# Threshold attention and a bilinear feed-forward layer on one core: two small VectorE instructions take a second tensor operand

## The chip, the cores and the metric

The kernel runs on one core of a Trainium2 chip. The metric is the device time of one execution in microseconds (us). A core has a matrix engine (TensorE, PE in the profile, with its weight loads listed as PEld), a vector engine (VectorE, DVE), a scalar engine (ScalarE, ACT), a general engine (GpSimd, POOL) and a queue engine that starts transfers (SyncE, SP). They run side by side and wait for each other through semaphores. Data lie in SBUF, an on-chip memory of 128 partitions, and matrix products arrive in PSUM. [...]

## The reference

The attention has 8 batches, 8 heads, 576 positions and a head width of 64. Scores that lie more than `tau` below the greatest of their row are dropped, and the rest go through a softmax. The heads of a position, side by side, are a row `x` of 512 numbers for the feed-forward layer.

```python
scores = scale * np.matmul(q, k.transpose(0, 1, 3, 2))
thresh = np.max(scores, axis=-1, keepdims=True) - tau
scores = np.where(scores >= thresh, scores, -1000000000.0)
scores = scores - np.max(scores, axis=-1, keepdims=True)
attn = np.exp(scores)
attn = attn / (np.sum(attn, axis=-1, keepdims=True) + 1e-09)
attn_out = np.matmul(attn, v)
x = attn_out.transpose(0, 2, 1, 3).reshape(B * S, H * D)
out = (x @ w_a) * (x @ w_b) @ w_out
```

Here x has 4608 rows, and the hidden width of the layer is 1536. All of it is float32.

## The kernel before

**Units of attention.** Heads are taken in 32 pairs. For each pair the 576 rows of queries are cut into units: four of 128 rows for each of the two heads, and a tail (u = 4) in which the last 64 rows of both heads share one tile of 128 partitions. So a unit u < 4 has two tiles of scores, a tail unit has one. There are 160 units, 128 with two tiles and 32 with one.

**What a unit does.** `scores` has TensorE compute q times k into PSUM (L352), VectorE take the maximum of each row (L359, one instruction for each tile, one number per partition) and then, once for the unit, the threshold `thr` (L360) from the one or two maxima and the constant `cut`. `cut` is a column of `scalars`: tau in the units of the raw product, or a huge number if tau is negative. `weigh` has ScalarE make a bias from the maximum (L379) and the exponential (L380), and VectorE keep those whose score reaches the threshold and add up the row (L383), which leaves the row sums in `sums`. `reciprocal` adds 1e-9 to the one or two sums, on ScalarE (L392) in the eight units beside which weights are being converted and on VectorE (L394) in the others, and takes the reciprocal (L396). For the first eight units the reciprocals become diagonal matrices for TensorE (`diagonals`, `turn_pe`). For the others ScalarE multiplies the weights by them (`normalise`, L402), VectorE transposes blocks of 32 by 32 (L446), SP writes them to a scratch tensor in HBM (`swap`, L457) and reads them back as `wT` (L466, L469), and TensorE multiplies by v (`product`, L483).

**The feed-forward layer.** Its matrix products (L633, L706, L763, L809) are cut into small steps by a generator, and `advance` puts as many of them between the parts of each unit as a pace allows. Some products are replaced by fewer ones over sums of blocks. GpSimd computes these sums from tiles in SBUF: L513 of x, L582 and L594 of the weights, L732 of the hidden values and of results. It also copies halves of x across partitions (L506) and multiplies hidden values (L599). In the first 150 us GpSimd and VectorE convert the weights as well (L254, L260, L268, L273).

**What sets the order.** The main loop over units writes the instructions in the order in which each engine is to run them, and `keep_order` ties every instruction to the one before it on its engine. Nothing is reordered by a scheduler. Every engine and the SP queue run strictly in that order. On VectorE the threshold stands behind the two maxima of its unit; behind it come transposes of the unit before and the masking. The sums stand in front of the reciprocal on which L402 waits.

**What touches the lines of the change.** `mx`, `thr`, `sums` and `rcp` are small tiles in SBUF of two float32 numbers per partition, each with two buffers. L360 reads `mx` and the scalar `cut`; L394 reads and writes `sums`. In a tail unit only the first column is used.

Of the kernel before, what the change touches and what calls it, by code (L numbers as in the profile page):

```python
# [14 lines left out]
ALU = mybir.AluOpType  # L15
# [37 lines left out]
def kernel(  # L53
# [38 lines left out]
    nc = tc.nc  # L92
# [33 lines left out]
    def banks(n, name):  # L126

        return psum.tile([P, 2, 512], FP32, tag="banks", name=name)[:, :, 0:n]
# [175 lines left out]
    ok, e_scale, e_nscale, cut, big = (scalars[:, c:c + 1] for c in range(5))  # L304
# [35 lines left out]
    def scores(i, u):  # L340
        qT, kT = prepared[i]["q" if i < HP else "q1" if u > 1 else "q0"], prepared[i]["k"]
        base = HALF if i >= HP and u > 1 else 0
        n = 2 if u < NT else 1
        sc = [banks(SH, "sc") for _ in range(n)]
        each = [(c, t, j) for c in range(2) for t in range(n) for j in range(2)]
        if units.index((i, u)) < BY_HEAD:
            each.sort(key=lambda x: x[2])
        for c, t, j in each:
            r = slice(j * D, (j + 1) * D)
            o = t if u < NT else 1 - j  # L350
            q0, to = (u * P + t * D if u < NT else MAIN) - base, slice(o * D, (o + 1) * D)
            nc.tensor.matmul(sc[j if u < NT else 0][to, c], qT[r, q0:q0 + D],  # L352
                             kT[r, c * SH:(c + 1) * SH], start=True, stop=True)
        mx = small.tile([P, 2], FP32, tag="mx", name="mx")
        thr = small.tile([P, 2], FP32, tag="thr", name="thr")
        bias = small.tile([P, 2], FP32, tag="bias", name="bias")
        for j in range(n):
            c = slice(j, j + 1)
            nc.vector.tensor_reduce(mx[:, c], sc[j], axis=AX.XY, op=ALU.max)  # L359
        nc.vector.tensor_scalar(thr[:, 0:n], mx[:, 0:n], cut, None, op0=ALU.subtract)  # L360
        scored[i, u] = (sc, thr, bias, mx)

    def rooms_of(i, u):
# [24 lines left out]
    def reciprocal(i, u, engine):  # L388
        ws, sums = weights[i, u]
        n = len(ws)  # L390
        if engine is nc.scalar:
            nc.scalar.activation(sums[:, 0:n], sums[:, 0:n], AF.Copy, bias=1e-9)  # L392
        else:
            nc.vector.tensor_scalar_add(sums[:, 0:n], sums[:, 0:n], 1e-9)  # L394
        rcp = small.tile([P, 2], FP32, tag="rcp", name="rcp")
        nc.vector.reciprocal(rcp[:, 0:n], sums[:, 0:n])  # L396
        weights[i, u] = (ws, rcp)
# [522 lines left out]
    n = 0  # L920
# [4 lines left out]
    for g in range(len(units) + PV_LAG):  # L925
# [4 lines left out]
        if here:  # L930
            i, u = units[g]
            scores(i, u)
# [24 lines left out]
        if here and g < BY_PE:  # L957
            reciprocal(i, u, nc.vector)
# [8 lines left out]
        if g > BY_PE:  # L967
            advance(PORTIONS[1] * pace)
            n = g - PV_LAG
# [12 lines left out]
        if here and g < BY_PE:  # L982
            diagonals(i, u)
        elif here:
            reciprocal(i, u, nc.scalar if converting else nc.vector)
            normalise(i, u)
# [71 lines left out]
```

## Time and profile before

| | before |
|---|---|
| median of 3 runs | 1462.98 us (1459.54 to 1463.87) |
| profiled execution, its own time | 1467.37 us |
| its span, first to last instruction | 1465.6 us |
| TensorE busy | 1387.9 us (95%) |
| VectorE busy | 1014.9 us (69%) |
| ScalarE busy | 682.9 us (47%) |
| GpSimd busy | 479.5 us (33%) |
| L360 on VectorE | 160 instructions, 44.4 + 6.9 us |
| L394 on VectorE | 152 instructions, 30.0 + 4.9 us |
| mean granted TensorE clock | 0.994 |

The profile is of one execution. Busy time is the time in which an engine ran an instruction, whatever the instruction waited for inside itself: a wait for a semaphore counts as idle, [...]. The two parts of L360 and L394 are those of two numbers per partition and of one. In a line of a group, `out<-in` names the tiles, and after the count come the busy time, the mean of one instruction in nanoseconds, and the idle time just before.

### The profile page before, as it was taken

How to read it: one execution, taken by the hardware profiler on the slowest of the kernel's cores; microseconds unless marked ns; L12 is line 12 of the kernel's file. 1: busy time of each engine (PE TensorE's matmuls, PEld its weight loads, DVE VectorE, ACT ScalarE, POOL GpSimd, SP SyncE). 2: the span in 40 equal slices, each digit the busy share in tenths (PEclk: the TensorE clock that was granted, in tenths of full speed). 3: DMA queues.
4: the chain of work that ended last, by engine and by line, in shares of the span. 5: the costliest groups of instructions: out<-in, count | busy, mean ns of one | idle time of the engine just before them, and what ended most of it. 6: DMA issues, size and time to landing. Idle time of an engine off the chain costs nothing.

```text
span 1465.6 us, 76332 instructions
## 1 busy us (share of the span) xinstructions
PE 1387.9 (95%) x34208; PEld 1248.2 (85%) x34208; DVE 1014.9 (69%) x2245; ACT 682.9 (47%) x1243; POOL 479.5 (33%) x668
## 2 busy tenths in 40 slices
PE   5788999999999999999999899999999999999998
PEld 4677687987989889899998788998898979989997
DVE  6898688787767787586757677767767776755223
ACT  5787455545545554454444445444545455431110
POOL 2774713423060606033334224150606060605000
PEclk9999999999999999999999999999999999999999
DMA  9976677668756775577555766477656776450000
GB/s 217 227 207 181 155 183 190 167 169 189 195 135 160 165 203 145 137 174 180 142 135 138 163 165 169 121 177 167 173 147 144 179 188 165 122 148 30 4 17 17
DMA packets 325080, 223.21 MB, mean 152 GB/s; under 512 B 169616, under 2 KB 308880, under 8 KB 324752
## 3 DMA queue, kind: packets, MB, share of 16 engines
q1 hardware_dynamic: 322384, 217.73, 60.7%
q8 instruction: 269, 4.41, 1.3%
q10 hardware_dynamic: 2368, 0.59, 0.2%
q14 instruction: 59, 0.48, 0.1%
HBM read 128.58 MB, written 89.65 MB: 149 GB/s over the span
## 4 chain that ended last, share of the span: by engine, by line
PE 78%; DVE 7%; DMA 5%; SPq 5%; issue 3%; ACT 1%; POOL 1%; ACTq 0%; DVEq 0%; POOLq 0%
PE pab L633 24%; PE pab L706 18%; PE po L763 17%; PE pv L483 9%; PE sc L352 9%; DMA wT<-swap 2%; SPq L457 2%; DVE mx L359 2%; SPq L147 1%; DMA qT<-in_q_dram 1%; DVE tw L446 1%; DVE tw L383 1%; PE po L809 1%; SPq L225 1%; POOL kept L732 0%
## 5 line engine op out<-in xcount | busy, mean ns | idle before, releaser
L402 ACT ACTIVATE tw<-tw,rcp 128x576 f32<-128x576 f32 x272 | 197.8, 769 | 216.9 <-DVE rcp L396 216.8
L359 DVE TENSOR_REDUCE mx<-sc 128x1 f32<-128x576 f32 x288 | 205.6, 751 | 134.6 <-PE sc L352 131.3
L380 ACT ACTIVATE tw<-sc,bias,scalars 128x576 f32<-128x576 f32 x288 | 239.3, 831 | 9.8 <-DMA vm<-in_v_dram 0.2
L599 POOL TENSOR_TENSOR h<-h,u 128x512 f32<-128x512 f32 x28 | 35.1, 1272 | 621.8 <-DVE h L676 485.8
L383 DVE SCALAR_TENSOR_TENSOR tw<-sc,thr,tw 128x576 f32<-128x576 f32 x288 | 223.0, 798 | 14.0 <-ACT tw L380 13.8
L763 PE MATMUL po<-wo_sb,h 64*64 64x256 f32 x3264 | 222.9, 377 | 0.0
L352 PE MATMUL sc<-kT,qT 64*64 64x288 f32 x2016 | 192.0, 405 | 10.5 <-ACT xt L490 4.7
L446 DVE STREAM_TRANSPOSE tw<-tw 128x576 f32<-128x576 f32 x272 | 196.0, 754 | 0.8 <-ACT tw L402 0.8
L483 PE MATMUL pv<-wT,vm 64*64 64x160 f32 (+3 forms) x5184 | 182.4, 275 | 14.3 <-DMA wT<-swap 8.0
L763 PEld LDWEIGHTS po<-wo_sb,h 64*64 64x64 f32 x3264 | 167.4, 133 | 24.9
L483 PEld LDWEIGHTS pv<-wT,vm 64*64 64x64 f32 x5184 | 166.2, 135 | 25.3 <-issue 10.4
L763 PE MATMUL po<-sums_u,h 64*64 64x256 f32 x2448 | 163.9, 376 | 1.6 <-DVE h L714 1.6
L732 POOL TENSOR_TENSOR h<-h 128x256 f32<-128x256 f32 x168 | 117.4, 728 | 114.6 <-PE po L763 100.5
L352 PEld LDWEIGHTS sc<-kT,qT 64*64 64x64 f32 x2016 | 115.1, 133 | 32.5 <-ACT xt L490 12.3
L763 PEld LDWEIGHTS po<-sums_u,h 64*64 64x64 f32 x2448 | 123.4, 133 | 20.7 <-DVE h L714 2.3
L633 PE MATMUL pab<-xU,wb_sb 64*64 64x128 f32 x4096 | 133.5, 270 | 0.2 <-issue 0.2
L379 ACT ACTIVATE bias<-mx,scalars 128x1 f32<-128x1 f32 x288 | 83.0, 288 | 100.6 <-DVE mx L359 100.5
L633 PEld LDWEIGHTS pab<-xU,wb_sb 64*64 64x64 f32 x4096 | 127.6, 133 | 2.6 <-issue 0.5
L491 DVE COPY xT<-pv 64x128 f32<-64x128 f32 (+1 forms) x136 | 38.1, 280 | 120.3 <-PE pv L483 119.1
L633 PE MATMUL pab<-xS,wa_sb 64*64 64x128 f32 x2048 | 110.8, 270 | 3.2 <-POOL xS L506 2.0
L490 ACT COPY xT<-pv 128x128 f32<-128x128 f32 (+1 forms) x68 | 17.6, 258 | 206.0 <-PE pv L483 205.9
L706 PE MATMUL pab<-xS,wb_sb 64*64 64x256 f32 (+1 forms) x1536 | 99.9, 359 | 2.9 <-issue 2.9
(137 smaller groups left out, 2429.0 us busy)
## 6 DMA issues: line engine op xcount, KB each, us to landing
swap<-tw SPq DMA_DIRECT2D x480, 144.0 KB, 2.6
wT<-swap SPq DMA_DIRECT2D x120, 576.0 KB, 4.7
vm<-in_v_dram SPq DMA_DIRECT2D x128, 72.0 KB, 3.3
swap<-tw SPq DMA_DIRECT2D x128, 72.0 KB, 2.0
kT<-in_k_dram SPq DMA_DIRECT2D x112, 72.0 KB, 4.3
wT<-swap SPq DMA_DIRECT2D x56, 144.0 KB, 2.9
out_dram<-kept SPq DMA_DIRECT2D x30, 256.0 KB, 4.0
qT<-in_q_dram SPq DMA_DIRECT2D x112, 40.0 KB, 4.5
```

The lines of the kernel that those rows point to most:

```text
L352: nc.tensor.matmul(sc[j if u < NT else 0][to, c], qT[r, q0:q0 + D], kT[r, c * SH:(c + 1) * SH], start=True, stop=True)
L359: nc.vector.tensor_reduce(mx[:, c], sc[j], axis=AX.XY, op=ALU.max)
L379: nc.scalar.activation(bias[:, j:j + 1], mx[:, j:j + 1], AF.Copy, scale=e_nscale)
L380: nc.scalar.activation(wb[j], sb[j], AF.Exp, bias=bias[:, j:j + 1], scale=e_scale)
L383: nc.vector.scalar_tensor_tensor(out=wv, in0=sb[j], scalar=thr[:, j:j + 1], in1=wv, op0=ALU.is_ge, op1=ALU.mult, accum_out=sums[:, j:j + 1])
L402: nc.scalar.activation(w, w, AF.Copy, scale=rcp[:, j:j + 1])
L446: nc.vector.transpose(w, w)
L483: nc.tensor.matmul(pv[c * D:(c + 1) * D, y], vm[rows, s], wT[y](rows, s), start=(s == 0), stop=(s == NSLOT - 1))
L633: nc.tensor.matmul(out[c * D:(c + 1) * D, r, f * P:(f + 1) * P], w[g][k][rows, w0:w0 + D], moving[k][rows], start=(fresh and k == 0 and f ...
L706: nc.tensor.matmul(pab[c * D:(c + 1) * D, r], w[rows, f // n, k, fs + c * D:fs + (c + 1) * D], moving, start=(k == 0), stop=(k == H - 1))
L732: (nc.vector if state["over"] else nc.gpsimd).tensor_tensor(*a, **kw)
L763: nc.tensor.matmul(po[c * D:(c + 1) * D, r, y], ht[rows, t0:t0 + D], other[rows, f], start=(f == 0), stop=(f == NF // 2 - 1))
```

## The change

The threshold and the sum plus 1e-9 are computed by `scalar_tensor_tensor` in place of `tensor_scalar`. That instruction computes (in0 op0 scalar) op1 in1. The second tensor operand is the same tile as the first. The threshold is min(mx − cut, mx), which is mx − cut because `cut` is not negative. The sum is max(sums + 1e-9, sums), which is sums + 1e-9. Both second operands lie in SBUF.

```diff
-        nc.vector.tensor_scalar(thr[:, 0:n], mx[:, 0:n], cut, None, op0=ALU.subtract)
+        nc.vector.scalar_tensor_tensor(out=thr[:, 0:n], in0=mx[:, 0:n], scalar=cut, in1=mx[:, 0:n],
+                                       op0=ALU.subtract, op1=ALU.min)
...
         if engine is nc.scalar:
             nc.scalar.activation(sums[:, 0:n], sums[:, 0:n], AF.Copy, bias=1e-9)
         else:
-            nc.vector.tensor_scalar_add(sums[:, 0:n], sums[:, 0:n], 1e-9)
+            nc.vector.scalar_tensor_tensor(out=sums[:, 0:n], in0=sums[:, 0:n], scalar=1e-9, in1=sums[:, 0:n],
+                                           op0=ALU.add, op1=ALU.max)
```

The lines that follow move down, L383 to L384, L396 to L398 and so on; the threshold stays at L360, and the sum becomes L395. Each engine has the same instructions in the same order as before, with the same semaphores.

## The prediction

> **What bounds the kernel now.** I read the page from the top: busy time by engine, then the chain of work that ended last. From it, these lines are the ones that matter here (microseconds busy, share of the span, instructions; then shares of the chain):
>
> ```profile
> span 1465.6 us, 76332 instructions
> PE 1387.9 (95%) x34208; PEld 1248.2 (85%) x34208; DVE 1014.9 (69%) x2245; ACT 682.9 (47%) x1243; POOL 479.5 (33%) x668
> ...
> PE 78%; DVE 7%; DMA 5%; SPq 5%; issue 3%; ACT 1%; POOL 1%; ACTq 0%; DVEq 0%; POOLq 0%
> ```
>
> TensorE sets the time: it is busy 95% of the span and is 78% of the chain. VectorE (DVE) has 31% of its span free and carries only 7% of the chain, some 100 us. A microsecond saved or added on DVE is therefore worth much less than a microsecond, except where the chain runs through it.
>
> The second view is DVE's groups with each shape apart (count, busy us, mean ns). The change rewrites the L360 and L394 groups; L396, L260 and L268 are there for comparison:
>
> ```profile
> L360 DVE TENSOR_SCALAR thr<-mx,scalars 128x2 f32<-128x2 f32 x128 | 44.4, 347 | 4.5
> L394 DVE TENSOR_SCALAR sums<-sums 128x2 f32<-128x2 f32 x120 | 30.0, 250 | 2.0
> L396 DVE RECIPROCAL rcp<-sums 128x2 f32<-128x2 f32 x128 | 21.2, 166 | 6.6 <-ACT sums L392 2.4
> L260 DVE SCALAR_TENSOR_TENSOR low<-raw,low 128x512 uint32<-128x512 uint32 x13 | 9.2, 709 | 0.1
> L268 DVE TENSOR_SCALAR wa_sb<-wa_sb 128x512 uint32<-128x512 uint32 x12 | 7.7, 639 | 0.0
> L360 DVE TENSOR_SCALAR thr<-mx,scalars 128x1 f32<-128x1 f32 x32 | 6.9, 214 | 1.1
> L394 DVE TENSOR_SCALAR sums<-sums 128x1 f32<-128x1 f32 x32 | 4.9, 154 | 1.0
> ```
>
> Two elements per partition cost 347 ns where one costs 214, and 250 where one costs 154. Width cannot explain that: the reciprocal costs 166 and 164 ns. The answer for L360's own instances gives 212/228/1849 ns as least, median and greatest, so most are short and some are very long.
>
> The third view is the order of time, DVE and GpSimd (POOL) side by side (start us, us). A long two-wide threshold, and a one-wide one in the same position:
>
> ```profile
> 268.90 1.85 DVE L360 TENSOR_SCALAR thr<-mx,scalars 128x2 f32<-128x2 f32 x1
> 268.36 4.69 POOL L594 TENSOR_TENSOR wb_sb<-wa_sb,wb_sb 128x1024 f32<-128x1024 f32 x2
> 784.14 0.21 DVE L360 TENSOR_SCALAR thr<-mx,scalars 128x1 f32<-128x1 f32 x1
> 782.40 2.49 POOL L599 TENSOR_TENSOR h<-h,u 128x512 f32<-128x512 f32 x2 [38.04 <-DVE h L676]
> ```
>
> The two-wide one starts in the first of two POOL instructions and ends at 270.75, just after that one ends (half of 4.69 us from 268.36 is 270.7). The one-wide one runs inside a POOL instruction and takes its plain 0.21 us. Going through all instances this way, 38 of the 128 two-wide thresholds and 35 of the 120 two-wide sums meet a running POOL instruction long enough to hold them. Together they last 15.2 and 10.8 us longer than their medians (228 and 168 ns): 26 us of DVE time. No one-wide instance is lengthened.
>
> [...] only the two-wide form waits. [...] the new form has two SBUF inputs. The trace has such instructions on DVE already:
>
> ```profile
> 100.74 1.12 DVE L260 SCALAR_TENSOR_TENSOR low<-sums_u,low 128x512 uint32<-128x512 uint32 x1
> 100.13 1.19 POOL L254 TENSOR_SCALAR wo_sb<-wo_sb 128x512 f32<-128x512 f32 x2
> 1332.11 7.56 DVE L732 TENSOR_TENSOR h<-h 128x256 f32<-128x256 f32 x9 [0.72 <-PE po L763]
> 1335.33 0.91 POOL L513 TENSOR_TENSOR xU<-xS 128x256 f32<-128x256 f32 x1
> ```
>
> L260 is the very instruction kind that the change uses. Undisturbed it takes 683 ns (its median); here it takes 1.12 us, and POOL's pair of instructions ends at 101.32. It waited 0.44 us, which is POOL's end (0.58 us after its start) less 0.14 us. Three other cases of L260 and twelve of L732 fit the same rule to within about 10 ns (L732: up to 950 ns for a plain 417). The present sums follow it too (1099 ns with POOL's end 1074 ns after the start: 931 waited, 143 less); the thresholds wait POOL's end less 0.20 us. [...] the waits of old and new form are alike.
>
> **The change part by part.** Counts: 160 thresholds (128 two-wide, 32 one-wide) and 152 sums (120 and 32). No instruction, wait or transfer is added or moved, and the order on every engine stays; the eight sums done on ScalarE (L392) are untouched.
>
> 1. *Plain cost.* [...] I take the new forms at these one-wide figures: 228 to 214 and 168 to 154, one-wide ones unchanged. That is 248 × 14 ns = 3.5 us less on DVE. Bounds: no gain below that is in sight; [...] If the second operand cost another 60 ns each, 312 × 60 = 19 us would be added to DVE.
> 2. *Waits of the two-wide forms.* They stay: 26 us before, 26 us after. Lower end: all 26 us go, if a two-element read slips past. I take the upper one, on L260 and L732.
> 3. *Waits of the one-wide forms.* New. Laying the rule (POOL's end less 0.20 us, less 0.14 us) on the one-wide instances of the trace, 11 thresholds would wait 5.2 us and 9 sums 4.6 us: 9.8 us more on DVE. Seven of them lie between 152 and 178 us behind the long POOL instructions L582, L594 and others, for 6.0 us; thirteen later ones have 3.8 us.
> 4. *What of it reaches the path.* Queued behind a late threshold are DVE's transposes (L446), for which a store and a load to `wT` wait, and the masking (L383). Behind a late sum are its reciprocal and ScalarE's L402. Cover: in 158 to 170 us the chain is TensorE's (L809), and DVE then idles 2.9 and 2.3 us waiting for TensorE, which takes in the 1.6 and 0.4 us. The 1.6 us at 173.43 meet idle spells of 1.3 and 1.1 us. The 1.6 us at 177.54 meet only 1.1 us, so 0.5 us may come through. The six late thresholds that have a wait of 0.27 us or more are followed within 7 us by 2.6 to 4.3 us of idle DVE; the six late sums, 1.2 us together, have no such spell close by, and I let half through: 0.6 us. Without any cover it would be 9.8 us. Against this, thr and sums make up some 26 pieces of the chain, each 14 ns shorter: −0.4 us.
>
> Sum: +0.5 + 0.6 − 0.4 = +0.7 us on the profiled execution's 1467.37 us. That execution stands 4.4 us above the median of the runs, 1462.98; on the median the forecast is 1463.5 us. Changes below 0.3%, which is 4.4 us, are about what a measurement of this kernel can tell from no change.
>
> **Rivals.** *The new form slips past GpSimd, and the 26 us go.* For it: the measured L260 and L732 have 256 and 512 elements, and no two-element instruction with two SBUF inputs is in the trace beside POOL work. Against it: their waits end at the other engine's end, not at a share of it. What would it give? The chain of work shows where waits now count:
>
> ```profile
> 129.64 0.62 DVE thr L360
> 489.57 0.70 DVE thr L360
> 964.70 0.74 DVE thr L360
> ```
>
> These hold 0.39, 0.47 and 0.51 us of waiting; with those at 44, 48, 51, 60, 81, 145 and 485 us the chain holds about 4 us. With some gain passed on by the earlier transposes I put it at −6 us: 1457 us, faster.
>
> *The one-wide waits land on the path.* The place is the one-wide tail units, above all those at 152 to 178 us, where a late sum delays ScalarE's L402 and then the transposes, stores and the product L483. Price: up to 9.8 us; it decides the sign from 4.4 us. For it: DMA and SPq are 10% of the chain, and they are fed by those transposes. Against it: the idle spells above. At half the price, 1468 us, slower.
>
> *A dearer instruction* (the 60 ns of part 1) would add 19 us to DVE, at DVE's 7% to 15% share of the path 1 to 3 us: no visible change.
>
> **Chances and range.** No visible change is likeliest, 0.70; the rival that gains 0.15; the one that loses 0.15. A gain beyond 4.4 us comes in seven tenths of the first rival, a loss beyond it in six tenths of the second, and 0.03 on each side comes from the main case, whose own range is 1459 to 1468 (the three runs shown already span 1459.5 to 1463.9). That makes faster 0.135, slower 0.12, same 0.745. The range for 8 in 10 reaches to about the middle of both rivals: 1457 to 1468.5 us.
>
> **What would show it.** In the groups of the changed kernel, both lines as SCALAR_TENSOR_TENSOR: two-wide thresholds still near 333 ns mean with a greatest over 1.5 us, two-wide sums near 236; one-wide thresholds up from 214 to about 214 + 5176/32 = 376, one-wide sums from 154 to about 299. DVE busy 1014.9 + 9.8 − 3.5 = 1021 us; TensorE's share unchanged. Two-wide means near 214 and 154 with no long instances, and DVE near 985 us, would make part 2 wrong and the gaining rival right; new waits for the threshold or the sums in the chain around 152 to 178 us would speak for the losing one.

## The result and the profile after

The changed kernel takes 1465.98 us (median of 21 runs, 1457.8 to 1474.19); the kernel before, run beside it, takes 1466.35 us (21 runs). The ratio is 1.0006 with a 95% interval of 0.999 to 1.0023: no change that can be told. (A ratio on record is not the quotient of the two medians, which would be 0.9997 here; in the experiments the two differ by up to 0.002.) In absolute terms 1465.98 us lies 2.5 us above the forecast of 1463.5 us, but the kernel before also has a median 3.4 us higher over its 21 runs than over the first three of them, on which the forecast stood. The profiled execution has a span of 1466.7 us, against 1465.6 us before.

The page of the changed kernel, first busy times and then the chain of work that ended last by engine:

```profile
span 1466.7 us, 76332 instructions
PE 1390.8 (95%) x34208; PEld 1248.7 (85%) x34208; DVE 1022.9 (70%) x2245; ACT 683.1 (47%) x1243; POOL 480.5 (33%) x668
...
PE 82%; DVE 7%; DMA 4%; issue 3%; SPq 2%; ACT 1%; POOL 1%; DVEq 0%; POOLq 0%; ACTq 0%
```

VectorE is busy 8.0 us longer (1014.9 to 1022.9), and its share of the chain is still 7%. VectorE's groups, each shape apart (count, busy us, mean ns), show where the 8 us are:

```profile
L360 DVE SCALAR_TENSOR_TENSOR thr<-mx,scalars 128x2 f32<-128x2 f32 x128 | 43.1, 337 | 4.5
L395 DVE SCALAR_TENSOR_TENSOR sums<-sums 128x2 f32<-128x2 f32 x120 | 28.5, 238 | 2.0
L360 DVE SCALAR_TENSOR_TENSOR thr<-mx,scalars 128x1 f32<-128x1 f32 x32 | 13.2, 412 | 1.1
L395 DVE SCALAR_TENSOR_TENSOR sums<-sums 128x1 f32<-128x1 f32 x32 | 9.4, 294 | 1.0
```

The two-wide forms went from 347 to 337 ns and from 250 to 238 ns: they still wait. The one-wide forms, which had not waited, went from 214 to 412 ns and from 154 to 294 ns. The order of time shows one such wait. It is the very threshold that ran undisturbed inside L599 before (here L601, two lines further down), followed by the two worst ones, beside long subtractions of weights on GpSimd:

```profile
786.22 0.77 DVE L360 SCALAR_TENSOR_TENSOR thr<-mx,scalars 128x1 f32<-128x1 f32 x1
784.48 2.50 POOL L601 TENSOR_TENSOR h<-h,u 128x512 f32<-128x512 f32 x2 [38.63 <-DVE h L678]
175.64 1.78 DVE L360 SCALAR_TENSOR_TENSOR thr<-mx,scalars 128x1 f32<-128x1 f32 x1
175.59 3.60 POOL L584 TENSOR_TENSOR wo_sb<-wo_sb 128x768 f32<-128x768 f32 x2
179.75 1.77 DVE L395 SCALAR_TENSOR_TENSOR sums<-sums 128x1 f32<-128x1 f32 x1
179.14 2.37 POOL L596 TENSOR_TENSOR first_u<-wb_sb 128x1024 f32<-128x1024 f32 x1
```

The first lasts until GpSimd's second instruction ends at 786.98; it took 0.21 us before. The second starts within 0.05 us of GpSimd's 1.8 us instruction and waits for all of it. Taking all instances, the rule of the prediction (GpSimd's end less 0.20 us for thresholds, less 0.14 us for sums), laid on this trace, gives waits of 5.4 us for ten one-wide thresholds and 4.3 us for ten one-wide sums; measured against the undisturbed medians (220 and 159 ns) they are 5.4 and 4.3 us. Two more one-wide thresholds, at 167.55 and 811.21 us, waited 0.21 and 0.58 us for a GpSimd instruction whose record starts 27 and 49 ns after theirs; the rule, which asks for a GpSimd instruction already running, leaves them out. For the two-wide ones it gives 14.0 and 10.4 us, and 13.7 and 10.3 us are measured.

Between 170 and 185 us, where two of the longest new waits lie, the chain of the changed kernel runs through TensorE (start us, us):

```profile
171.69 2.13 PE pv L485 x66
174.79 2.68 PE pab L708 x51
178.25 0.90 PE pv L485 x59
181.13 3.88 PE pab L708 x71
```

TensorE has products of the layer to work on while VectorE waits. Neither wait is in the chain of this execution, and none of the other twenty lengthened one-wide instructions is.

### The profile page after: what moved, and what is told of

It is laid out like the page before. It is cut to its first block, busy times and chain, and to the rows that moved or that the text cites. A ratio compares the mean times of both kernels' runs of the same rounds, so it can differ in the third digit from the quotient of the medians.

```text
span 1466.7 us, 76332 instructions
## 1 busy us (share of the span) xinstructions
PE 1390.8 (95%) x34208; PEld 1248.7 (85%) x34208; DVE 1022.9 (70%) x2245; ACT 683.1 (47%) x1243; POOL 480.5 (33%) x668
## 4 chain that ended last, share of the span: by engine, by line
PE 82%; DVE 7%; DMA 4%; issue 3%; SPq 2%; ACT 1%; POOL 1%; DVEq 0%; POOLq 0%; ACTq 0%
PE pab L635 26%; PE po L765 19%; PE pab L708 18%; PE sc L352 10%; PE pv L485 9%; DVE mx L359 1%; DMA wT<-swap 1%; DMA qT<-in_q_dram 1%; DVE tw L448 1%; DVE tw L384 1%; SPq L459 1%; PE po L811 1%; POOL kept L734 1%; PE tp L429 1%; DMA raw<-in_moe_w_a_dram 0%
## 5 line engine op out<-in xcount | busy, mean ns | idle before, releaser
L359 DVE TENSOR_REDUCE mx<-sc 128x1 f32<-128x576 f32 x288 | 205.6, 751 | 135.8 <-PE sc L352 132.6
L601 POOL TENSOR_TENSOR h<-h,u 128x512 f32<-128x512 f32 x28 | 35.1, 1276 | 621.5 <-DVE h L678 484.8
L384 DVE SCALAR_TENSOR_TENSOR tw<-sc,thr,tw 128x576 f32<-128x576 f32 x288 | 222.9, 798 | 13.2 <-ACT tw L381 13.0
```

The source lines that it names most:

```text
L384: nc.vector.scalar_tensor_tensor(out=wv, in0=sb[j], scalar=thr[:, j:j + 1], in1=wv, op0=ALU.is_ge, op1=ALU.mult, accum_out=sums[:, j:j + 1])
```

## Experiments

Two theories were set against each other. A: the second operand in SBUF makes the one-wide instructions wait for GpSimd, the two-wide ones wait as before, and TensorE's work covers nearly all of it. B: VectorE's waits land in the time. A kernel's ratio is to the kernel before, run on the same chip in the same session, with its 95% interval.

### The change by width

The new form in the tail units alone is the kernel `one_wide`, and in the others alone `two_wide` (with `n == 2`). The diff is that of `one_wide`; its sums are treated the same way:

```diff
-        nc.vector.tensor_scalar(thr[:, 0:n], mx[:, 0:n], cut, None, op0=ALU.subtract)
+        if n == 1:
+            nc.vector.scalar_tensor_tensor(out=thr[:, 0:n], in0=mx[:, 0:n], scalar=cut, in1=mx[:, 0:n],
+                                           op0=ALU.subtract, op1=ALU.min)
+        else:
+            nc.vector.tensor_scalar(thr[:, 0:n], mx[:, 0:n], cut, None, op0=ALU.subtract)
...
```

> Only the tail units (one number per partition) have the new form; the two-wide thresholds and sums stay as before. Theory A (the second SBUF operand makes the one-wide instructions wait for GpSimd, and the waits are covered): one-wide thresholds rise from 214 to about 400 ns mean, one-wide sums from 154 to about 295 ns, VectorE busy from 1015 to about 1025 us, two-wide groups unchanged (347 and 250 ns), ratio of times 0.998 to 1.002. Rival B (waits of VectorE land on the path): the 10 us come out in the time, ratio 1.005 to 1.007.

> Only the units with two numbers per partition have the new form; the tail units stay as before. Theory A: two-wide thresholds 337 ns, sums 238 ns (plain 221 and 160 ns, the waits for GpSimd as before), one-wide ones at 214 and 154 ns with no waits, VectorE busy about 1012 us, ratio 0.998 to 1.002. Rival B: 3 us less, ratio 0.998, not to be told from A here. A rival by which the new form has other waits of its own would show in other means.

VectorE's groups of `one_wide`, then of `two_wide`:

```profile
L364 DVE TENSOR_SCALAR thr<-mx,scalars 128x2 f32<-128x2 f32 x128 | 43.6, 341 | 4.5
L361 DVE SCALAR_TENSOR_TENSOR thr<-mx,scalars 128x1 f32<-128x1 f32 x32 | 12.8, 400 | 1.1
L399 DVE SCALAR_TENSOR_TENSOR sums<-sums 128x1 f32<-128x1 f32 x32 | 8.2, 257 | 1.0
```

```profile
L361 DVE SCALAR_TENSOR_TENSOR thr<-mx,scalars 128x2 f32<-128x2 f32 x128 | 44.0, 343 | 4.5
L399 DVE SCALAR_TENSOR_TENSOR sums<-sums 128x2 f32<-128x2 f32 x120 | 28.4, 236 | 2.0
L364 DVE TENSOR_SCALAR thr<-mx,scalars 128x1 f32<-128x1 f32 x32 | 6.9, 214 | 1.1
```

`one_wide`: ratio 0.9989 (0.9973 to 1.0006), VectorE busy 1022.3 us. `two_wide`: ratio 0.9991 (0.9976 to 1.0006), VectorE busy 1015.1 us, where 1012 was expected. So nearly all of the added busy time belongs to the one-wide form (7.4 us in `one_wide`, 0.2 us in `two_wide`), and it costs no time that can be measured: B's 1.005 to 1.007 lies outside the interval. The one-wide sums rose to 257 ns, less than the 295 ns expected.

That TensorE covers a given wait does not hold in every execution. The threshold at 175.64 us, which lasts 1.78 us in the changed kernel and is not on the chain there, lasts as long in the profiled execution of `one_wide`, beside the same subtraction on GpSimd, and here it is on the chain:

```profile
173.73 1.79 DVE thr L361
```

Thresholds and sums together hold 13.1 us of that chain, against 6.2 us in the kernel before, and the time is not longer. The length that an instruction has on the chain of one execution is therefore not its price in time.

### With waits and without, at the same number of instructions

Old form and new form, each two-wide instruction written as two one-wide ones. The old form of width one has not waited in any trace so far; the new form could wait twice. `split_ts`, and `split_stt` likewise with `scalar_tensor_tensor`; the sums are treated the same way:

```diff
-        nc.vector.tensor_scalar(thr[:, 0:n], mx[:, 0:n], cut, None, op0=ALU.subtract)
+        for j in range(n):
+            nc.vector.tensor_scalar(thr[:, j:j + 1], mx[:, j:j + 1], cut, None, op0=ALU.subtract)
...
```

> The old one-source form, but every two-wide threshold and sum is written as two one-wide instructions, which takes away the waits for GpSimd and adds 248 instructions. Theory A: no instance is lengthened; thresholds 320 x about 210 ns less what overlaps, VectorE busy about 1030 us (1015 - 26 + 248 instructions of 154 to 214 ns), ratio 0.998 to 1.003. Rival B: the removed 26 us of waits and the added 44 us of instructions count alike: ratio about 1.012.

> The new form, every two-wide threshold and sum written as two one-wide instructions: as many instructions as the kernel with the old form split, but each of them can wait for GpSimd. Theory A: the first of a pair waits as the two-wide one did, the second may wait again for the next GpSimd instruction where those follow each other; VectorE busy 1065 to 1090 us, yet against the split old form the time is the same within 0.4%. Rival B: 35 to 60 us longer than the split old form, 2.4 to 4%.

The groups of `split_ts`, then those of `split_stt`:

```profile
L361 DVE TENSOR_SCALAR thr<-mx,scalars 128x1 f32<-128x1 f32 x288 | 49.3, 208 | 1.1
L396 DVE TENSOR_SCALAR sums<-sums 128x1 f32<-128x1 f32 x272 | 30.9, 144 | 2.0
```

```profile
L361 DVE SCALAR_TENSOR_TENSOR thr<-mx,scalars 128x1 f32<-128x1 f32 x288 | 87.1, 338 | 1.1
L397 DVE SCALAR_TENSOR_TENSOR sums<-sums 128x1 f32<-128x1 f32 x272 | 50.7, 218 | 2.0
```

The same pair of thresholds in the order of time, first in `split_ts` with GpSimd's work beside it, then in `split_stt`:

```profile
267.74 0.33 DVE L361 TENSOR_SCALAR thr<-mx,scalars 128x1 f32<-128x1 f32 x2
267.53 4.71 POOL L596 TENSOR_TENSOR wb_sb<-wa_sb,wb_sb 128x1024 f32<-128x1024 f32 x2
```

```profile
271.22 4.08 DVE L361 SCALAR_TENSOR_TENSOR thr<-mx,scalars 128x1 f32<-128x1 f32 x2
270.62 4.66 POOL L598 TENSOR_TENSOR wb_sb<-wa_sb,wb_sb 128x1024 f32<-128x1024 f32 x2
```

The pair takes 0.33 us in the old form, in the midst of GpSimd's work, and 4.08 us in the new one, where it ends with the second of GpSimd's two instructions (275.30 and 275.28). In `split_ts` no threshold is over 216 ns; in `split_stt` the longest takes 2402 ns.

It is not the kind of instruction as such that waits. The masking is a `scalar_tensor_tensor` too, but only one of its two tensor operands, `tw`, lies in SBUF; the other, `sc`, is in PSUM. In the changed kernel (ns as least, median and greatest):

```profile
L384 DVE SCALAR_TENSOR_TENSOR tw<-sc,thr,tw x288: 768/806/821, 15.5 to 1307.3; 128x576 f32<-128x576 f32 x144
```

Of its 288 instances 37 start while a GpSimd instruction has more than 300 ns to go, and none is lengthened.

`split_ts` has a ratio of 0.9977 (0.9962 to 0.9992), and VectorE busy 1000.6 us. This is less than the 1030 us expected, in the main because an instruction starts before the one in front of it has ended: the 288 thresholds of 208 ns, 59.9 us in all, are only 49.3 us busy. `split_stt` has a ratio of 1.0084 (1.0061 to 1.0107), and VectorE busy 1054.5 us, where 1065 to 1090 us were expected. Against each other, the medians are 1479.74 and 1465.8 us: 13.9 us for 53.9 us of VectorE's busy time, about a quarter. Nearly all of the 53.9 us are waits: what exceeds 220 and 165 ns (a little above the undisturbed medians of 212 and 154 ns) is 35.8 us for the thresholds and 17.6 us for the sums of `split_stt`, and nothing in `split_ts`. Both expectations missed: A had the two within 0.4% of each other, B had 2.4 to 4%. Waits of this size are no longer covered throughout. The chain of `split_stt` has long ones on it:

```profile
242.19 2.28 DVE thr L361
271.30 1.71 DVE thr L361
273.04 2.26 DVE thr L361
885.56 1.27 DVE sums L397 x2
```

None of these is on the chain of the kernel before at such a length. Added over the chain, thresholds hold 13.8 us in `split_stt`, 4.1 us before and 2.2 us in `split_ts`. This fits the longer time, though `one_wide` shows that such a sum alone does not prove it.

### VectorE's time without a wait

> The 1e-9 is left out, on VectorE and on ScalarE: the reciprocal is taken of the sums themselves, which are at least 1, so that float32 gives the same number. VectorE loses 152 instructions with 35 us, of them 11 us of waits for GpSimd. Theory A (VectorE's time is mostly covered by TensorE): VectorE busy about 980 us, ratio 0.996 to 1.000. Rival B: ratio about 0.976.

In `no_sum` the addition is left out:

```diff
-        if engine is nc.scalar:
-            nc.scalar.activation(sums[:, 0:n], sums[:, 0:n], AF.Copy, bias=1e-9)
-        else:
-            nc.vector.tensor_scalar_add(sums[:, 0:n], sums[:, 0:n], 1e-9)
         rcp = small.tile([P, 2], FP32, tag="rcp", name="rcp")
```

VectorE's busy time falls to 980.0 us as expected, and the ratio is 1.0007 (0.999 to 1.0023). 35 us of VectorE's work, 11 us of them waits, are worth nothing that can be measured. B's 0.976 is excluded.

### Which waits are on the chain

The two splits alone, in the old form.

> Old one-source form; only the two-wide threshold is written as two one-wide instructions, the sums stay as before. Theory A1 (the waits of the thresholds are those that lie on the chain, some 3 of its 4 us): no threshold is lengthened, sums at 250 ns, ratio 0.997 to 0.999, as with both split. Rival A2 (the waits of the sums are those that count): ratio 0.999 to 1.001.

> Old one-source form; only the two-wide sum is written as two one-wide instructions, the thresholds stay as before. Theory A1: no sum is lengthened, thresholds at about 345 ns, ratio 0.999 to 1.001. Rival A2: ratio 0.997 to 0.999, as with both split.

`thr_split`: ratio 0.9965 (0.9952 to 0.9979), 1460.04 us against 1464.41 us. `sum_split`: ratio 0.9996 (0.9981 to 1.001). Taken by themselves the two fit A1, with a little more for the thresholds than it gave them, and nothing that can be measured for the sums. `thr_split_no_sum` below, in which the thresholds do not wait either, speaks against it. The thresholds' group in `thr_split` is that of `split_ts`, 49.3 us busy and none over 216 ns; the waits of the sums are left:

```profile
L395 DVE TENSOR_SCALAR sums<-sums 128x2 f32<-128x2 f32 x120 | 28.4, 237 | 2.0
```

This version is faster than the kernel before by about a third of a per cent; it was not run beside the changed kernel.

### Attempts at more

> The row maxima lie in unused columns of the scores' own PSUM tile in place of an SBUF tile, so that the old form of the threshold has no SBUF tensor input; the sums stay as before. Theory A: no threshold is lengthened by GpSimd, its mean falls from 320 to about 220 ns (15 us less), the sums stay at 250 ns; the second maximum waits for the first, some 50 to 100 ns for each of 128 units; VectorE busy about 1005 to 1012 us, ratio 0.997 to 1.002. Rival B: 15 us less, ratio 0.990.

```diff
-        sc = [banks(SH, "sc") for _ in range(n)]
+        full = [psum.tile([P, 2, 512], FP32, tag="banks", name="sc") for _ in range(n)]
+        sc = [t[:, :, 0:SH] for t in full]
...
-        mx = small.tile([P, 2], FP32, tag="mx", name="mx")
+        mx = full[0][:, 0, SH:SH + 2]
```

`psum_ts` takes 1492.4 us, a ratio of 1.0155 (1.0133 to 1.0177). Of what was expected, one half holds: two-wide thresholds fall to a mean of 219 ns. None of the thresholds is over 221 ns, where the old two-wide form with its source in SBUF took up to 1849 ns: with the source in PSUM it does not wait for GpSimd. The time does not fall, and a new wait came in. The waits of `psum_ts` (us in total, times, longest us):

```profile
ACT bias L380 <- DVE thr L361: 179.4, 125, 4.7
```

In the kernel before, the bias on ScalarE waited for the maximum (100.5 us in total). With the maxima in the tile of the scores, it waits for the threshold, and so for both maxima, before the first exponential can start. VectorE's busy time is 1026.6 us, not the 1005 to 1012 expected; the maxima alone, which now follow each other without overlap, are 220.1 us busy where they were 205.6 (113 ns more for each of the 128 units with two). That the wait of the bias is what lengthens the run is likely from its size, and no run shows it alone. As a test of what the waits for GpSimd cost, this run is spoilt.

> Both: maxima in PSUM and the 1e-9 left out (the same number in float32), so that neither small instruction waits for GpSimd: all 26 us of such waits go, and 152 instructions. Theory A: VectorE busy about 970 to 978 us; the first 150 us, where the chain runs through VectorE, gain some 4 us, ratio 0.994 to 0.999. Rival B: 40 us less, ratio 0.973.

This is `psum_ts` with the 1e-9 left out as well, and it has the same new wait: 1.0087 (1.0063 to 1.0112), VectorE busy 993.9 us, so that the expectation missed. Against `psum_ts` it is 9.5 us faster by the medians (1482.92 and 1492.4 us) for 32.7 us less of VectorE's time, while 35 us less gained nothing that can be measured in `no_sum`: what VectorE's time is worth differs between these two kernels.

> The two-wide threshold as two one-wide instructions, and the 1e-9 left out (the sums are at least 1, so that float32 gives the same number): all waits for GpSimd go, and 152 instructions with them. Theory A1: VectorE busy about 970 us; the gain is that of the thresholds alone, since leaving out the sums gave nothing, ratio 0.996 to 0.999. If what the two give adds up with the 24 us of other VectorE time, 0.994 or less.

`thr_split_no_sum` has a ratio of 0.9992 (0.9975 to 1.0009), just outside A1's 0.996 to 0.999, and VectorE busy 972.6 us. It removes more of VectorE's work than `thr_split`, its thresholds do not wait either (216 ns at most), and it gains less: run in the same session, its mean time is 3.4 us longer than that of `thr_split` (95% interval 1.0 to 5.7 us). So the gain of `thr_split` cannot be put down to the waits of the thresholds alone. Why it goes when the sums are left out is open; that any small shift of VectorE's instructions moves the time by some microseconds is a rival that no run here excludes.

## Why the prediction was right

1. *Plain cost.* 228 to 214 and 168 to 154 ns were taken. The undisturbed medians after are 221 and 160 ns two-wide, and 220 and 159 ns one-wide, where 214 and 154 had been taken. So the saving was about 7 to 8 ns and not 14, and the one-wide forms cost 5 to 6 ns more than before. The dear bound, 60 ns each (the difference of 214 and 154 ns between the one-wide threshold and the one-wide sum before), did not come. That the new forms would cost what the old one-wide ones do was the author's estimate.
2. *Two-wide waits stay.* All that exceeds the undisturbed median adds up to 26.0 us before and 25.2 us after (14.9 + 10.3). The rival by which a two-element read slips past GpSimd has fallen. Why the old form waits at a width of two and not of one, no run shows.
3. *One-wide waits.* 5.2 + 4.6 us forecast by laying the rule on the old trace, 5.4 + 4.3 us found by that rule, and 10.5 us with everything above the median; 11 and 9 instances forecast, 10 and 10 found, and the two thresholds outside the rule. VectorE's busy time was to be 1021 us and is 1022.9 us: +10.5 for these waits, −0.8 for the two-wide ones and about −1.5 for the plain cost make +8.2 us, against the 8.0 measured. `one_wide` shows that these are nearly the whole of the increase.
4. *What reaches the path.* +0.7 us was forecast; the ratio's interval, −1.5 to +3.4 us, holds it. It leaves out the losing rival's full 9.8 us and also its half price. For the one-wide waits alone the forecast was +0.5 + 0.6 = +1.1 us, and `one_wide` gives −4.0 to +0.9 us, so that even this was, if anything, too much. Which wait would come through, and which be covered, was not borne out: 0.5 us was given to the sum at 177.54 us and nothing to the threshold at 173.43 us, and it is the latter that turns up on a chain, in `one_wide`. That the cover is TensorE's work was argued from the chain between 170 and 185 us of one execution; `no_sum` supports it from the other side. The added sum, +0.7 us on the median of 1462.98 us, would make 1463.7 us where 1463.5 us was written. That the absolute time of 1465.98 us lies in the range owes something to the range's width: the kernel before moved by 3.4 us with no change at all.

The losing rival had a true mechanism at the wrong price: `split_stt` shows that waits of this very kind do land in the time, at a quarter of their length, in a kernel where two thresholds or sums in a row can wait for two GpSimd instructions in turn. The prediction's estimate that some 4 us of threshold and sum waits lie on the old chain is too high. It counts in full the waits of the thresholds at 44, 60 and 81 us, of which the chain holds only 0.07, 0.07 and 0.04 us; what the chain holds of waiting is at most 2.9 us. What removing the waits gains is not settled: 0.23% (3.4 us) in `split_ts`, 0.35% (5.1 us) in `thr_split`, and nothing that can be measured in `thr_split_no_sum`.

## What to carry to other kernels

An instruction that is long only now and then (here 228 ns at the median and 1849 ns at most), and whose neighbour in width or form never is (216 ns at most), may be waiting inside itself: lay the other engine's instructions beside it in the order of time. Giving a small instruction a second SBUF operand did not free it from GpSimd here: the two-wide forms waited 25.2 us where they had waited 26.0, and the one-wide ones, which had not waited, 10.5 us. What did free the old form was a width of one, even at twice the number of instructions (no threshold over 216 ns in `split_ts`), or a source in PSUM (none over 221 ns in `psum_ts`). Whether the freed time is worth anything is another question: 35 us less on VectorE gained nothing that can be measured in `no_sum`.

## What was not expected of the hardware

Two one-wide thresholds in a row cost less than twice one: 0.33 us for a pair of 0.21 us each. The pair still costs more than an undisturbed two-wide threshold (0.23 us), but with its waits gone the split form is the cheaper in VectorE's busy time (1005.7 us in `thr_split`, 1014.9 us before). And two such instructions with two SBUF operands in a row wait for GpSimd twice: the pair of 4.08 us. Nor does it always help VectorE to start first: the thresholds at 167.55 and 811.21 us of the changed kernel waited for a GpSimd instruction whose record starts 27 and 49 ns later.
